# Float64 remainder bits on ScalarE, one-column softmax scaling in batch 0, and a new instruction order, in an attention and two-layer feed-forward kernel

## The chip, the cores and the metric

The kernel runs on one core of a Trainium2 chip. TensorE (PE) multiplies matrices; VectorE (DVE), ScalarE (ACT) and GpSimd (POOL) do elementwise work; SyncE (SP) issues all DMA transfers of this kernel. The metric is the device time of one execution in microseconds (us), lower being better; the median of several runs counts.

## The reference

Attention with a memory term, then two feed-forward blocks on its output. The sizes are B, H, S, D = 4, 8, 576, 64; 2304 tokens of width 512; a hidden width of 2048.

```python
scores = np.where(causal, -1e9, np.matmul(q, k.T) / sqrt(D))
a = np.exp(scores - scores.max(-1)); a /= a.sum(-1) + 1e-9
local = np.matmul(a, v)
q_p = phi(q)                       # where(x > 0, x, exp(x) - 1) + 1
mem_out = (q_p @ M_prev) / (q_p . z_prev + 1e-6)
x = g * mem_out + (1 - g) * local  # g = sigmoid(beta), per head
h = x @ moe_w_in                   # 512 -> 2048
x = where(h >= 1, h, where(h <= -1, 0, (h + 1)**2 / 4)) @ moe_w_out
h = x @ moe2_w_in
out = (max(h, 0) + alpha * min(h, 0)) @ moe2_w_out
```

The four weight matrices arrive as 64-bit floats, the scaled ones with bits beyond float32.

## The kernel before

**Precision.** The products of the feed-forward blocks run on pairs of float16: a value is split into a high and a low half, and each product is three matmuls (`mm_in`, `mm_out`). Batch 0's attention runs wholly in float32 (`plain`); its softmax weights are transposed on TensorE and copied out of PSUM into `tt`. Batches 1 to 3 split the weights into float16 pairs `p` and transpose them with a DMA (`pt<-p` in the profile). The score products `s` run in float32 in all batches, and the products after the transposes are `px`.

**Weights.** `Weights.groups` handles one of four groups of a matrix (w1i, w1o, w2i, w2o). It loads four tiles of 512 64-bit words per partition (part `a`, 512 KB each), takes maxima and scales (part `m`), and makes a float32 value of each word (parts `0` to `3`): a Prelu on ACT makes `t` from the upper 32-bit word, the lower word is shifted right by 29, and a third operation on DVE joins both. Parts `s0` and `s1` split `t` into float16 halves. `raw[:, :, 1]` is the upper word and `raw[:, :, 0]` the lower one. w2o takes another path (`flips`) that the change does not touch. The raw tiles of w1i lie in four buffers (`ring`); the float16 halves of w1o take the same four buffers afterwards. The raw tiles of w1o use buffers of tag `x` and `g`.

**Softmax.** In `attend` DVE takes the running minimum `mxt` of the negated scores into `e`, ACT makes the exponentials with their row sums `sm` (two columns, one for each head of a pair), and DVE multiplies `sm + 1e-9` with `g1i` (batch 0) or `cs` and takes the reciprocal. `p` or `pf` is `e` times that.

**Order.** Nothing is issued as written. Each call is recorded as an operation in a `Plan`; `schedule` plays the operations on modelled engines and emits them in the order of their modelled starts, engine by engine. Each engine then executes its own list in order. Among ready operations the one comes first whose section stands earlier in the list `RANK`. Section names are short: `p0` prepares batch 0, `a1C2` is the attention of batch 1, blocks C (all five), head pair 2, and `a1C2.3` its part for query block 3; `w1i0.a` are the loads of the first group of w1i; `u00` and `d00` are the first block's up and down products (`up1`, `down1`) of batch 0, chunk 0; `f00` is the second block (`ffn2`). An operation recorded with `either` may run on one of several engines: the planner keeps it on the first unless another one finishes it sooner by more than `SLACK`, or the dictionary `HOME` names the engine. `HOME` is empty before. A key is the section and the count of `either` calls in it. `Plan.cost` has a duration for each operation; `two_ports` tells which DVE operations are planned as excluding GpSimd:

```python
big = [a for a in ins if a.space != PSUM and mybir.dt.size(a.dtype) == 4 and math.prod(a.shape[1:]) > 1]
...
return method in ("tensor_tensor", "scalar_tensor_tensor") and len(big) > 1
```

All lines of the program go through a helper, so the profile puts them all at L423 (the call in `run`); tile names tell them apart.

Of the kernel before, what the change touches and what calls it, by code (L numbers as in the profile page):

```python
# [1200 lines left out]
a0A0.x2 a1C2.2 a1C2.4 u01.7 a1C2.3 a1C1.4 a1C1.3 u01.0 p1.0 d00.o3 a1C3.1 a1C1.2 p1.3 d00.o2 a1C1.0 u01.4 a1C1.1
a1C3.2 a1C3.0 u01.1 p2.0 u01.5 u01.6 a1C3.4 p2 a2C0.1 d01.o0 a1C3.3 d01.o2 a2C1.1 u10.0 d01.o1 p2.s a2C0.2 a2C1.4
a2C1.0 a2C0.q a2C1.2 w1o2.1 a2C1.3 a2C3.4 p2.1 u10.4 a2C0.3 p2.3 a2C0.0 a1C1.x4 a2C0.4 u10.6 a2C2.0 u10.7 a2C3.3
d01.o3 u10.2 a2C2.2 w1o1.3 a1C2.x4 a2C3.0 a2C3.2 a2C3.1 u10.5 u11.1 w1o2.s0 a2C2.1 u10.1 a3C0.0 a2C2.4 a2C2.3 u10.3
a0A3.x2 u11.3 a3C0.4 w1i2.a u11.6 p3.s a3C0.1 a3C0.2 d10.o0 a3C1.0 a3C1.2 w1o2.3 d10.o1 a1C1 d10.o2 a3C1.1 w1i0.s0
d10.o3 u11.2 a3C0.3 d21 w1o3.s1 u11.0 u11.5 u11.4 u11.7 d11.o0 m2.2 a2C2.x4 a0A3.q a3C1.3 a3C1.4 u20.1 u20.5 w1i3.1
a3C0.x2 d11.o2 a3C3.q d11.o1 a3C3.3 u20.4 a3C1.q d11.o3 a3C2.x2 w1i1.a s1 a3C3.4 a3C1 w2i0.a u20.0 u20.7 u20.3 u20.2
a1C2.q w1o0.0 u20.6 d20.o0 w2i0.s1 a3C1.x2 a3C2.1 d20.o2 a3C2.4 u21.2 w1o3.0 a3C2.3 u21.7 w2i0.3 a3C2.x4 a3C3.1 a3C3.2
a1C2 w2i2.a w2i0.m w1o1.2 a3C0.q a3C2.2 m3.1 u21.4 a3C2.0 a3C3.0 m2.1 d20.o1 p2.2 a1C3 w2i1.a w2i2.m d20.o3 w1o0.2
u21.3 a0A2.q w2i2.s0 w1i1.0 u21.0 a0B2.x4 u21.1 w2i2.s1 a2C1 w2i0.1 a3C3.x4 w2i2.1 u21.5 u21.6 w2i1.3 w2i3.0 d21.o2  # L1210
# [75 lines left out]
```

## Time and profile before

| | |
|---|---|
| median of 3 runs | 1060.23 us (1058.87 to 1060.51) |
| profiled execution | 1059.26 us |
| its span, first to last instruction | 1057.4 us |
| TensorE, DVE, ACT, GpSimd busy in the span | 953.8, 691.7, 560.9, 311.5 us |
| mean granted TensorE clock | 0.984 of full speed |

The profiled execution is one run with a record of each instruction. The span is 1.9 us shorter than its time, which holds what lies before the first and after the last instruction. Busy times are unions over an engine's instructions, and the stages have different limits, so the span has to be read stage by stage.

### The profile page before, as it was taken

How to read it: one execution, taken by the hardware profiler on the slowest of the kernel's cores; microseconds unless marked ns; L12 is line 12 of the kernel's file. 1: busy time of each engine (PE TensorE's matmuls, PEld its weight loads, DVE VectorE, ACT ScalarE, POOL GpSimd, SP SyncE). 2: the span in 40 equal slices, each digit the busy share in tenths (PEclk: the TensorE clock that was granted, in tenths of full speed). 3: DMA queues.
4: the chain of work that ended last, by engine and by line, in shares of the span. 5: the costliest groups of instructions: out<-in, count | busy, mean ns of one | idle time of the engine just before them, and what ended most of it. 6: DMA issues, size and time to landing. Idle time of an engine off the chain costs nothing.

```text
span 1057.4 us, 20522 instructions
## 1 busy us (share of the span) xinstructions
PE 953.8 (90%) x8043; PEld 712.8 (67%) x8043; DVE 691.7 (65%) x1777; ACT 560.9 (53%) x1099; POOL 311.5 (29%) x315
## 2 busy tenths in 40 slices
...
PEclk9999978999999999999999999999999999999999
...
GB/s 314 295 117 103 82 139 124 82 150 138 169 114 139 118 176 123 92 115 175 100 148 199 32 139 69 125 61 68 57 34 7 18 12 12 18 12 18 7 17 24
DMA packets 132097, 104.24 MB, mean 99 GB/s; under 512 B 98464, under 2 KB 113312, under 8 KB 132000
## 3 DMA queue, kind: packets, MB, share of 16 engines
...
q14 instruction: 34, 0.28, 0.1%
...
## 4 chain that ended last, share of the span: by engine, by line
PE 44%; DVE 4%; DMA 3%; ACT 1%; POOL 1%; issue 0%; ACTq 0%; SPq 0%; DVEq 0%; POOLq 0%
PE h L423 21%; PE o L423 17%; PE y L423 5%; DMA w2i_raw<-in_w2i 2%; DMA pt<-p 1%; DVE u L423 1%; PE px L423 1%; PE s L423 0%; DMA w2o_raw<-in_w2o 0%; DVE w2o L423 0%; ACT u L423 0%; POOL d L423 0%; POOL g L423 0%; DVE w2i_t L423 0%; DVE p L423 0%
## 5 line engine op out<-in xcount | busy, mean ns | idle before, releaser
L423 PE MATMUL h<-x,w1i 128*128 128x288 f16 x1536 | 202.8, 288 | 4.8 <-ACT u L423 3.4
L423 PE MATMUL y<-g,w1o 128*128 128x288 f16 x1536 | 204.2, 288 | 1.9 <-DVE ysc L423 1.8
L423 PE MATMUL o<-g,w2o 128*128 128x288 f16 x1536 | 194.7, 286 | 1.3 <-ACT u L423 0.7
L423 PE MATMUL h<-yt,w2i 128*128 128x288 f16 x1536 | 195.3, 286 | 0.1
L423 PEld LDWEIGHTS <-w1i 128*128 128x128 f16 x1536 | 147.2, 98 | 55.6 <-issue 18.0
L423 PEld LDWEIGHTS <-w1o 128*128 128x128 f16 x1536 | 146.8, 98 | 52.4 <-issue 12.8
L423 PEld LDWEIGHTS <-w2o 128*128 128x128 f16 x1536 | 150.3, 98 | 39.7 <-issue 1.9
L423 PEld LDWEIGHTS <-w2i 128*128 128x128 f16 x1536 | 150.1, 98 | 38.0 <-issue 0.3
L423 DVE SCALAR_TENSOR_TENSOR u<-u,al 128x288 f32<-128x288 f32 x128 | 66.5, 546 | 121.6 <-ACT u L423 121.5
L423 POOL TENSOR_TENSOR g<-u,g 128x576 f16<-128x576 f32 x49 | 73.4, 1501 | 211.7 <-ACT yt L423 92.9
L423 DVE TENSOR_TENSOR g<-u,g 128x576 f16<-128x576 f32 x79 | 66.7, 846 | 85.7 <-ACT g L423 85.2
L423 ACT ACTIVATE e<-e,mxt 128x64 f32<-128x64 f32 (+4 forms) x160 | 88.2, 552 | 56.0 <-DVE mxt L423 51.9
L423 PE MATMUL s<-qk 64*128 64x288 f32 (+4 forms) x384 | 90.6, 492 | 27.7 <-DVE mxt L423 12.9
L423 ACT ACTIVATE u<-h,sa 128x288 f32<-128x288 f32 x128 | 59.3, 498 | 104.6 <-PE h L423 101.3
L423 ACT ACTIVATE g<-u 128x576 f16<-128x576 f32 x117 | 79.3, 679 | 63.6 <-DVE u L423 39.9
L423 DVE SCALAR_TENSOR_TENSOR p<-e,sm,p 128x320 f16<-128x320 f32 (+4 forms) x119 | 74.1, 658 | 13.1 <-POOL p L423 7.0
L423 PEld LDWEIGHTS s<-qk 64*128 64x128 f32 x384 | 40.4, 208 | 51.8 <-DVE mxt L423 21.6
L423 DVE SCALAR_TENSOR_TENSOR u<-u,c,d 128x576 f32<-128x576 f32 x64 | 62.6, 980 | 15.2 <-ACT d L423 8.2
L423 DVE CUSTOM_DVE_ANT_0 e<-s,mask 128x64 f32<-128x64 f32 (+4 forms) x160 | 64.7, 419 | 5.4 <-PE s L423 5.1
L423 ACT ACTIVATE u<-h,bu,su 128x576 f32<-128x576 f32 x64 | 52.7, 823 | 20.5 <-PE h L423 14.6
L423 ACT ACTIVATE oe<-o,osc 128x288 f32<-128x288 f32 x32 | 16.0, 499 | 85.8 <-PE o L423 85.8
L423 ACT ACTIVATE d<-h,bu,sd 128x576 f32<-128x576 f32 x64 | 52.6, 821 | 4.9 <-PE h L423 4.8
(215 smaller groups left out, 1142.3 us busy)
## 6 DMA issues: line engine op xcount, KB each, us to landing
...
```

The source lines that it names most:

```text
L423: fn(*args, **kw)
```

## The change

A fourth constant `half` is made at the start. The new helper `rest_of` records the shift of the lower word as an operation for DVE or ACT: on ACT, the upper 16 bits of the lower word (a number below 65536) are multiplied by 2^-13, and 2^-14 - 0.5 is added, so that rounding to a whole number leaves the upper three bits, which is what the shift by 29 leaves. It is used for w1i, w1o and w2i. In batch 0 the scaling of `sm` is done for one column at a time. In the planner the rate of DMA transposes goes from 292 to 215 KB per us. `RANK` is replaced, and `HOME` gets 661 entries; of these, 33 concern `rest_of` (keys such as `w1i0.1:1`). The diff, with `RANK` and `HOME` cut to the lines that name the loads of w1i0 and w1o0 and these keys:

```diff
--- before.py
+++ after.py
@@ -15,6 +15,7 @@
 BF16 = mybir.dt.bfloat16
 I16 = mybir.dt.int16
 I32 = mybir.dt.int32
+U16 = mybir.dt.uint16
 AF = mybir.ActivationFunctionType
 ALU = mybir.AluOpType
 AX = mybir.AxisListType.X
@@ -392,7 +393,7 @@
                 busy[eng] = True
                 if eng == "dma":
                     hw = max(hw, now) + (0.625 if op.wide else 0.45)
-                    dma = max(dma, hw + 0.65) + (op.size / 360e3 if op.size > 0 else -op.size / 292e3)
+                    dma = max(dma, hw + 0.65) + (op.size / 360e3 if op.size > 0 else -op.size / 215e3)
                     if op.size < 0:
                         hw = max(hw + 0.57, dma - 0.92)
                     post(max(hw, dma - 3.0), free, eng)
@@ -563,6 +564,8 @@
         base=0,
         channel_multiplier=1,
     )
+    half = const.tile([P, 1], F32, name="half")
+    G.memset(half, 2.0**-14 - 0.5)
     gt = const.tile([P, H], F32, name="gt")
     g1i = const.tile([P, H], F32, name="g1i")
     Q.dma_start(out=gt, in_=beta.partition_broadcast(P))
@@ -593,6 +596,25 @@
             else:
                 out.append([w[:, k] for k in range(2)])
         return out
+
+    def rest_of(raw):
+
+
+        low = raw[:, :, 0]
+
+        def on_act():
+            A.activation(
+                out=low,
+                in_=raw.rearrange("p n t -> p (n t)").bitcast(U16).rearrange("p (n t) -> p n t", t=4)[:, :, 1],
+                func=AF.Identity,
+                scale=2.0**-13,
+                bias=half,
+            )
+
+        def on_dve():
+            V.tensor_scalar(out=low, in0=low, scalar1=29, scalar2=None, op0=ALU.logical_shift_right)
+
+        plan.either(on_dve, on_act)
 
     class Weights:
 
@@ -671,9 +693,7 @@
                     A.activation(out=t[:, i], in_=top.bitcast(F32), func=AF.Prelu, scale=2.0**-112, alpha=-(2.0**32))
 
                     if self.flips is None:
-                        V.tensor_scalar(
-                            out=raw[:, :, 0], in0=raw[:, :, 0], scalar1=29, scalar2=None, op0=ALU.logical_shift_right
-                        )
+                        rest_of(raw)
                     else:
                         rest3 = raw[:, :, 0].rearrange("p (f e) -> p f e", e=64)
                         V.scalar_tensor_tensor(
@@ -853,14 +873,16 @@
                     bias=mxt[:, h : h + 1],
                     accum_out=sm[:, h : h + 1],
                 )
-            V.scalar_tensor_tensor(
-                out=sm,
-                in0=sm,
-                scalar=1e-9,
-                in1=(g1i if plain else cs)[:, 2 * pr : 2 * pr + 2],
-                op0=ALU.add,
-                op1=ALU.mult,
-            )
+
+            for h in ((0, 1), (1, 2)) if plain else ((0, 2),):
+                V.scalar_tensor_tensor(
+                    out=sm[:, slice(*h)],
+                    in0=sm[:, slice(*h)],
+                    scalar=1e-9,
+                    in1=(g1i if plain else cs)[:, 2 * pr + h[0] : 2 * pr + h[1]],
+                    op0=ALU.add,
+                    op1=ALU.mult,
+                )
             V.reciprocal(out=sm, in_=sm)
             nq = P if bk else 64
             if plain:
@@ -1193,39 +1215,121 @@
 ORDER = _order()
 
 RANK = """
-s3 w1i1.1 a0A1.2 p0.1 a0A2.x2 w1i0.2 w1i0.3 m1.0 p0.s u00.0 w1i0.0 a0A1.1 w1i0.1 w1i1.m s0 a0A1.0 w1i1.s1 p0.0 w1i0.s1
-a0A0.1 c a0A1.q w1i2.1 w1i0.m a0A2.1 a0A0.q w1i2.s1 a0A0.0 p0.3 a0A2.0 a0A0.2 l p0.2 w1i2.m a0A2.2 w1o0.1 m1.3 a0A3.1
-a0A3.0 a0A3.2 a0B0.3 w1i3.m p0 p1 u00.3 w1o0.a w1o2.a u00.4 u00.5 u00.1 u00.2 a0B2.q w1o0.m w1o2.m w1o1.a u00.6 u00.7
...
-f10.4 f10.0 f10.3 f10.5 w2i3.1 w2o0.3 f11.6 w2o2.s1 a0B3 w1i0.a f10.6 f10.7 a1C1.q w2o2.3 f11.7 f11.2 t1 f10.o1
...
+w1i0.m w1i1.3 u00.0 m1.0 w1i0.s0 s0 a0A1.q d00 p0.1 w1i0.s1 a0A0.x2 w1i0.1 a0A1.0 a0A1.1 a0A0.1 p0.3 a0A0.q a0A3.q
+w1i0.a a0A0.0 p0.s w1i1.m a0A1.2 a0A0.2 a0A2.1 a0A2.0 w1i0.0 l w1i2.m a0A2.2 m1.3 p0 a0A3.0 w1o0.a w1i1.1 a0A3.1
+a0A3.2 p1 a0B0.3 w1i3.m w1i2.s1 p0.2 u00.1 w1o2.a w1o0.m u00.5 a0A3 w1o2.m w1o1.a w1i2.1 u00.7 u00.2 u00.3 w1o3.a p0.0
+u00.4 u00.6 a0B0.4 p1.2 a0B2.4 a1C0 a0B1.4 d00.o1 w1o3.m w1o0.1 w1o1.m p1.1 w1i3.0 a0B1.3 a0B2.3 a0B3.3 w1o2.s1 a0B3.4
...
 """.split()
 
-HOME = {}
+HOME = dict(
+    x.split("=")
+    for x in """
+w1i0.0:1=dve w1i0.1:1=act w1i0.s0:1=act w1i0.s0:2=dve w1i0.2:1=dve w1i0.3:1=act w1i0.s1:1=pool w1i0.s1:2=pool
...
+a0A0.x2:3=act w1i1.1:1=act w1i1.2:1=act w1i1.s1:2=pool a0A1.0:1=pool a0A1.0:2=act a0A1.0:4=act a0A1.1:1=act
+a0A1.1:4=act a0A1.2:2=act a0A1.2:3=dve a0A1.x2:1=act a0A1.x2:3=act w1i2.0:1=act w1i2.s0:1=pool w1i2.s0:2=dve
+w1i2.2:1=act w1i2.s1:1=pool w1i2.s1:2=dve a0A2.0:1=dve a0A2.0:3=pool a0A2.0:4=act a0A2.1:1=pool a0A2.1:2=pool
+a0A2.1:3=dve a0A2.2:1=act a0A2.2:2=pool a0A2.2:3=dve a0A2.2:4=act a0A2.x2:1=act w1i3.0:1=act w1i3.s0:2=dve
+w1i3.3:1=act w1i3.s1:1=act w1i3.s1:2=dve a0A3.0:1=dve a0A3.0:2=dve a0A3.0:3=pool a0A3.1:1=pool a0A3.2:2=dve
...
+u00.6:3=dve u00.7:1=act w1o0.0:1=dve w1o0.1:1=act w1o0.s0:2=dve w1o0.2:1=dve w1o0.3:1=dve w1o0.s1:1=dve w1o1.0:1=act
+w1o1.1:1=act w1o1.s0:2=pool w1o1.2:1=act w1o1.3:1=act w1o1.s1:1=pool w1o1.s1:2=dve w1o2.0:1=act w1o2.s0:1=pool
+w1o2.2:1=dve w1o2.3:1=dve w1o2.s1:1=pool w1o2.s1:2=dve w1o3.0:1=act w1o3.1:1=dve w1o3.s0:2=dve w1o3.2:1=act
...
+u21.5:3=pool u21.6:1=dve u21.6:2=act u21.7:1=act u21.7:3=dve w2i0.0:1=dve w2i0.2:1=act w2i0.3:1=act w2i0.s1:2=dve
+w2i1.1:1=act w2i1.s0:1=pool w2i1.s1:2=dve w2i2.0:1=dve w2i2.1:1=dve w2i2.2:1=dve w2i2.s1:2=dve w2i3.0:1=act
+w2i3.s0:1=act w2i3.s0:2=dve w2i3.3:1=dve w2i3.s1:1=act w2i3.s1:2=dve u30.0:2=act u30.0:3=dve u30.1:1=pool u30.1:2=pool
...
+""".split()
+)
 
 
 # ---- launch: one core; the host only lays the arrays out ----
```

## Rows read from the trace of the kernel before

**Rows 1.** The page: busy us, share of the span, count; TensorE's granted clock in slices.

```profile
PE 953.8 (90%) x8043; PEld 712.8 (67%) x8043; DVE 691.7 (65%) x1777; ACT 560.9 (53%) x1099; POOL 311.5 (29%) x315
...
PEclk9999978999999999999999999999999999999999
```

**Rows 2.** Stretches: length, busy us of PE, PEld, DVE, ACT, POOL; clock, DMA share, GB/s.

```profile
13.00:50.00 37.00, 10.53 (x48) 6.87 (x48) 32.69 (x99) 10.22 (x22) 9.76 (x8) 1.00 0.95 332
50.00:200.00 150.00, 114.57 (x741) 77.66 (x742) 132.94 (x367) 106.41 (x208) 77.84 (x69) 0.90 0.35 112
128.00:164.00 36.00, 23.77 (x136) 15.03 (x134) 29.16 (x91) 25.60 (x44) 17.37 (x16) 0.72 0.43 141
200.00:603.00 403.00, 379.51 (x3614) 272.08 (x3613) 325.15 (x939) 265.70 (x562) 180.65 (x208) 1.00 0.59 131
500.00:603.00 103.00, 99.46 (x886) 74.17 (x884) 83.64 (x189) 69.90 (x127) 42.39 (x40) 1.00 0.49 124
603.00:1057.40 454.40, 447.71 (x3640) 355.73 (x3637) 197.23 (x358) 171.80 (x296) 40.76 (x24) 1.00 0.13 42
```

**Rows 3.** TensorE's groups: count, busy us, mean ns, idle us before them, releasers.

```profile
L423 PE MATMUL s<-qk 64*128 64x288 f32 (+4 forms) x384 | 90.6, 492 | 27.7 <-DVE mxt L423 12.9 <-DMA qk<-in_qk 7.7 <-DVE w1o_t L423 3.4
L423 PE MATMUL px<-pt,vh 128*64 128x128 f16 (+1 forms) x1080 | 40.3, 219 | 15.1 <-DMA pt<-p 12.0 <-DVE x L423 1.4 <-PE h L423 0.7
L423 PE MATMUL pt<-ident,pf 128*128 128x128 f32 x120 | 24.4, 354 | 17.4 <-ACT pf L423 12.3 <-POOL pf L423 5.0
L423 PE MATMUL px<-tt,vf 128*64 128x128 f32 (+1 forms) x240 | 23.0, 337 | 8.0 <-ACT tt L423 5.7 <-ACT e L423 2.3
```

**Rows 4.** DVE's groups by shape: batch 0's scaling of `sm`, the three shifts by 29.

```profile
L423 DVE SCALAR_TENSOR_TENSOR sm<-sm,g1i 128x2 f32<-128x2 f32 x20 | 10.2, 509 | 2.5 <-ACT e L423 2.3
...
L423 DVE TENSOR_SCALAR w1o_raw<-w1o_raw 128x512 int32<-128x512 int32 x16 | 7.9, 492 | 1.8 <-DMA w1o_raw<-in_w1o 1.8
...
L423 DVE TENSOR_SCALAR w2i_raw<-w2i_raw 128x512 int32<-128x512 int32 x16 | 7.5, 471 | 0.2 <-DMA w2i_raw<-in_w2i 0.2
L423 DVE TENSOR_SCALAR ring<-ring 128x512 int32<-128x512 int32 x16 | 7.2, 455 | 1.0 <-DMA ring<-in_w1i 0.9
```

**Rows 5.** ACT's groups by shape: plain copy, bias from a tile, Prelu of raw words.

```profile
L423 ACT ACTIVATE g<-u 128x576 f16<-128x576 f32 x117 | 79.3, 679 | 63.6 <-DVE u L423 39.9 <-PE o L423 21.3 <-PE y L423 2.2
...
L423 ACT ACTIVATE d<-d,c 128x576 f32<-128x576 f32 x51 | 39.3, 771 | 0.7
...
L423 ACT ACTIVATE w1i_t<-ring 128x512 f32<-128x512 f32 x16 | 10.5, 666 | 9.0 <-POOL w1i L423 4.8 <-DMA ring<-in_w1i 2.4 <-DVE w1i L423 1.8
```

**Rows 6.** The tiles `sm` and `mx`: operation, count, ns min/median/max, first and last start.

```profile
L423 DVE SCALAR_TENSOR_TENSOR sm<-sm,g1i x20: 145/157/2068, 11.2 to 183.7; 128x2 f32<-128x2 f32 x20
...
L423 DVE TENSOR_TENSOR mx<-rm,sq x16: 147/156/1044, 17.0 to 425.4; 128x1 f32<-128x1 f32 x16
```

**Rows 7.** The timeline: start us, duration us, around three of these operations.

```profile
59.31 2.13 POOL L423 TENSOR_TENSOR w1i<-w1i_t,w1i 128x1024 f16<-128x1024 f32 x1
...
59.53 1.93 DVE L423 SCALAR_TENSOR_TENSOR sm<-sm,g1i 128x2 f32<-128x2 f32 x1
...
63.52 0.14 DVE L423 SCALAR_TENSOR_TENSOR sm<-sm,g1i 128x2 f32<-128x2 f32 x1
63.59 0.21 DVE L423 CUSTOM_DVE_ANT_0 e<-s,mask 128x64 f32<-128x64 f32 x1
...
421.87 1.55 POOL L423 TENSOR_TENSOR g<-u,g 128x576 f16<-128x576 f32 x1 [0.66 <-ACT g L423]
...
422.40 1.04 DVE L423 TENSOR_TENSOR mx<-rm,sq 128x1 f32<-128x1 f32 x1
```

**Rows 8.** The DMA issues: count, median us from issue to landing.

```profile
pt<-p SPq DMA_TRANSPOSE x60, 4.3
```

**Rows 9.** The timeline of SP, which issues the transfers.

```profile
5.56 4.12 SPq L423 DMA_DIRECT2D w1o_raw<-in_w1o  x5
...
10.40 0.55 SPq L423 DMA_DIRECT2D ring<-in_w1i  x1
```

More of the change, by code (lines that the diff above doesn't have):

```diff
@@ L1201 @@
[L1201 to L1210, printed above, removed]
@@ new lines @@
+a1C2.2 u01.1 a1C2.4 a1C2.1 a1C3.1 d00.o3 w1i3.3 a1C3.0 s3 a1C1.1 a1C1.0 a1C3.2 a1C1.2 a2C0.1 p1.3 d10 w1o0.3 a1C3.4
+a0B1 a1C3.3 w1o1.s0 w1o2.1 d00.o2 u01.4 u01.0 p2.s u01.6 d01.o1 w1i1.s0 u01.5 w1i1.s1 d01.o0 a2C1.2 a2C1.1 u10.4
+a2C1.0 w1o1.2 a2C0.2 a2C1.3 a2C1.4 a2C0.4 a2C0.3 d01.o3 a2C3.3 a2C3.0 d01.o2 a2C0.0 u10.6 a2C3.4 u10.1 u10.0 a2C2.1
+a2C3.2 u10.2 a2C3.1 u10.3 a2C2.0 w1o1.0 p2.0 u10.5 u11.1 u10.7 d10.o0 a2C2.4 d10.o1 a2C2.2 a2C2.3 w1o3.2 a3C0.0 a3C1.3
+u11.6 m3.0 d10.o2 u11.3 a3C0.1 p3.s w1o0.0 a3C1.4 w1i3.s1 d10.o3 d21 u11.5 w1o3.s0 u11.7 a3C0.2 w2i0.0 m3.2 u11.0
@@ new lines @@
+a3C0.x4 a3C1.0 u11.2 u11.4 d11.o0 d11.o1 m1.2 w2i0.a a0B2.x4 a3C0.4 a3C0.3 w1i1.0 d11.o3 u20.3 a3C3.4 a3C1.1 u20.4
+w1i0.2 m3.1 a3C1.2 a1C2.q w1i3.s0 p2 a3C2.2 a1C2 a3C1 w1i2.3 u21.2 a3C2.1 w2i0.1 a3C3.q d11.o2 a2C0.q u20.7 a0B2
+a3C2.x2 m1.1 u20.0 w2i0.s1 a2C0.x2 a3C2.4 m2.1 a3C3.3 u21.3 w2i2.s1 a0A2.x2 a3C2.0 u20.5 w1i2.s0 d11 u20.1 a3C3.1
+w2i0.m a3C1.x2 u20.2 u21.7 a3C2.x4 a2C0.x4 u20.6 a3C0.q a3C3.0 a2C2.q w2i2.0 a2C1.q u21.4 d20.o0 d20.o3 p2.3 w1i0.3
+w1o3.s1 d20.o1 u21.5 d20.o2 a3C3.2 a1C1 a1C0.x2 u21.1 w2i2.a a3C2.3 w2i1.s0 w2i3.3 u21.0 u21.6 w2i2.m d21.o0 w2i1.s1
@@ new lines @@
+w2i1.a d21.o1 u30.1 d21.o2 a1C1.x4 d21.o3 u30.0 u30.6 u31.2 w2i2.2 m3.3 w2i3.a w1o1.1 w2i2.s0 w2i1.2 w2i3.s0 w1i3.a
+f01 u30.4 w2i3.m c u30.2 u30.7 a2C3.x2 u30.3 m2.2 u31.1 w1o1.3 w2o3.a w1o2.3 w2i2.1 p2.1 w2i1.m u30.5 w2o0.1 u31.5
+d30.o2 d30.o0 w2o3.m f00 w1o0.s0 w2o0.a d30.o1 d30.o3 w2o3.3 a1C3 w2o3.2 u31.0 a2C0 w2i1.3 w2o0.m w2i3.2 w2o1.m u31.7
+w1o2.2 p2.2 a3C1.q u31.3 u31.4 f00.2 f00.3 u31.6 f00.7 a2C1 d31.o1 f00.6 w2o2.2 s1 d31.o0 w2o0.s0 d31.o3 w2o3.s0
+d31.o2 w2o3.s1 w1i2.a f00.1 a2C3 w1o1.s1 a2C2 w1o3.3 f00.4 f00.0 a0A0 f01.7 f00.5 f01.5 f01.6 p3.1 d01 d30 f00.o1
```

93 lines of the change are left out of this document (77 added, 16 removed).

## The prediction, as put on record before the changed kernel was timed

> **What bounds the kernel now.** I read the page first. TensorE is busy for 953.8 of the 1057.4 us, so 103.6 us are idle; VectorE (DVE) comes second with 65%, and the granted clock is at full speed except in a few slices [rows 1]. An average over unlike stages says little, so the stages come next. From 603 us to the end TensorE is idle for only 454.4 - 447.7 = 6.7 us: nothing but fewer matmuls could shorten that part, and the change removes none. Between 200 and 603 it is idle for 23.5 us, between 50 and 200 for 35.4 us, and between 13 and 50 for 26.5 us [rows 2]. A gain has to come out of the first 603 us, mostly out of the first 200. There DVE is busy for 32.69 + 132.94 = 165.6 of 187 us, which is 0.89, while ScalarE (ACT) is at 106.4 of 150, which is 0.71 after 50 us. So up to 200 us DVE is nearly the bound; at 500 to 603 us TensorE is. The worst hole is 128 to 164 us: 12.2 us idle, at a mean granted clock of 0.72, so part of it ran at the lower of the two levels, 1.2 GHz [rows 2]. Third, the groups of TensorE with the idle time before them say what was late: score products wait for DVE's running minima, the transposes of batch 0 for ACT (12.3 us), the products after a DMA transpose for that transpose (12.0 us), and those after a copy out of PSUM for ACT (8.0 us) [rows 3].
>
> **The change part by part.** The sum is made against the profiled execution, 1059.3 us; the median of the runs shown is 1.0 us above it.
>
> *The shift on ACT.* `rest_of` may run on DVE or on ACT; 48 tiles pass through it, 16 each of w1i, w1o and w2i. The list `HOME` pins 33 of them: 8 on ACT and 2 on DVE for w1i, 8 and 6 for w1o, 4 and 5 for w2i; the planner chooses for the other 15, with DVE as the home it leaves only for a clear gain. I count the 20. On DVE one takes 455, 492 and 471 ns by mean [rows 4], so 8 x 0.455 + 8 x 0.492 + 4 x 0.471 = 9.4 us leave DVE. With none of the free 15 on DVE it would be 14 x 0.455 + 10 x 0.492 + 11 x 0.471 = 16.5 us. On ACT the new operation has no row. The nearest is the Prelu of the same 512 words at 666 ns, and a bias read from a tile adds 771 - 679 = 92 ns at equal width [rows 5]: 0.76 us each, 15.2 us in all, bounds 0.67 (a free bias) to 0.85 (twice that addition). What is this worth on the path? The 16 of w1i and w1o (7.6 us of DVE) stand before 200 us, where DVE is 0.89 busy: 7.6 x 0.89 = 6.7 us gained. The four of w2i fall where TensorE idles 3.5 of 103 us [rows 2]; the full TensorE queue hides them, and without that cover they would bring their 1.9 us. Against it stand 16 x 0.76 = 12.2 us more on ACT. Operations queued behind them are the copies for which TensorE waits; such waits (12.3 + 8.0 us, the latter partly the exponentials) fill about 20.3 of 150 us, so I charge 12.2 x 0.135 = 1.7 us. Net: -5.0 us. Bounds: -6.7 with ACT's room hiding all, +12.2 with every one in front and no relief on DVE.
>
> The Trainium skill ("ScalarE: Activation LUTs", Rules for kernel authors) sends adds and products to VectorE and not to ScalarE. By that rule the exchange costs 0.76 - 0.47 us of engine time per tile, 5.8 us over the 20; the sum would have +5.8 in place of -5.0. The rule looks at an engine alone; here the engine it prefers is the fuller one.
>
> *One column at a time.* The scaling of the softmax sums of batch 0 becomes two instructions of one column for one of two. That is 20 more on DVE. An unhindered one took 0.14 us and let the next operation begin 0.07 us after its own start [rows 7], so 20 x 0.07 x 0.89 = +1.2 us, and with 0.15 each +2.7. Can it bring something? The 20 take 145 ns at least, 157 at the median and 2068 at most; with a mean of 509 (10.2 us over 20) they hold 20 x (509 - 157) = 7.0 us too much [rows 4, 6]. Four long ones (1.5 to 2.07 us) carry nearly all of it, each beside a GpSimd operation: the one at 59.53 ended with GpSimd's product of 59.31 [rows 7]. If one column ended these stalls, 7.0 x 0.89 = 6.3 us would come back. But the trace has an operation with two inputs of one column, `mx<-rm,sq`. It has a median of 156 ns and once took 1044: it began at 422.40 and ended at 423.44, while GpSimd's product began at 421.87 and ended at 423.42 [rows 6, 7]. So one column waited for GpSimd too. I take 0 for the gain, with -6.3 as the other end.
>
> The Trainium skill ("SBUF — State Buffer", Who interferes with whom) says that a DVE instruction with two SBUF inputs contends with a GpSimd instruction that reads SBUF, and names no width below which it does not. By that rule the sum keeps +1.2; the planner's own test in `two_ports` leaves out operands of one column, and by that the sum would have 1.2 - 6.3. The long `mx` is on the rule's side.
>
> *Landing times.* The 60 DMA transposes are 12 of each of five block lengths, 131 KB times 1 to 5, so 393 KB on average. The planner had 0.625 + 0.65 + 393/292 + 0.8 = 3.4 us for it, and now has 393/215 instead: 3.9 us. The trace has 4.3 us from issue to landing [rows 8]. The plan was 0.9 us short and is now 0.4 us short, so it should put more other work before the products. The waits are 12.0 us; a bit over half would be 6, and I take -5.0, as other work has to be found for each; bounds 0 to -12.0.
>
> *New order.* `w1i0.a` now ranks before `w1o0.a`. Before, five loads of w1o (512 KB each) left SP's queue from 5.56 us, and the first of w1i followed at 10.40 [rows 9]; nothing needs w1o until the first `down1`. What stands behind them in SP's queue moves too: the loads of `vc`, from which `prepare` takes its scale, then find four loads of w1i ahead of them in place of five of w1o, about as much. Five loads at the 332 GB/s of this stretch [rows 2] are 7.9 us; DVE idles only 4.3 us there, so I take -2.0, bounds 0 to -4.3. All other places in `RANK` and the pins in `HOME` have no row: the plan is a list from a model, and a step that is put behind a late one delays all behind it in its in-order queue. I take 0, between -12.2 (the hole at 128 us filled) and the same on the other side (a second hole of that size).
>
> **Sum:** -5.0 + 1.2 - 5.0 - 2.0 = -10.8 us. 1059.3 - 10.8 = 1048.5; with the 1.0 us to the median, 1049 us. A difference under 0.2% (2.1 us) counts as none: single runs lie 1.6 us apart.
>
> **The rivals.** *The split works* (chance 0.10): one column escapes GpSimd, 1049 - 6.3, about 1043 us. For it: 16 of 20 sums did not stall at all, so a new place may do the same. Against: the long `mx`.
>
> *The hole closes* (0.15): the new order brings `down1` of batch 0 into the stretch at 128 to 164 us. The hole holds 12.2 us of idleness, and 0.28 x 23.8 = 6.7 us went to the clock; half of the 18.9 us gives about 1040 us. For it: the low clock lies in the hole itself, so work put there would pay twice. Against: DVE is 0.81 busy there and w1o itself has to be prepared by it.
>
> *Nothing arrives* (0.10): ACT takes what DVE gives, and the transposes were covered only in name; 1060 us. For it: the freed DVE time is under 6% of the first 200 us. The Trainium skill's rule above (ScalarE: Activation LUTs) points here: with its +5.8 the sum ends at 1060.3 us.
>
> *ACT becomes the bound* (0.20), the other side: the moved shifts stand ahead of the copies `tt`, `pf` and of the drains of `h`, between 98 and 164 us where ACT is already 0.71 busy. The whole +12.2 us counts and the relief of DVE brings nothing: 17.2 us more than my sum, 1067 us. It decides as soon as about eight of the 16 stand in front of an awaited copy (8 x 0.76 = 6.1 us, without relief), because the other three terms, 1.2 - 5.0 - 2.0 = -5.8, are then outweighed.
>
> **How the numbers follow.** My sum has 0.42 and a range of its own of 1041 to 1057; 0.03 stay for larger shifts. Faster: 0.42 + 0.10 + 0.15 and a little of "nothing arrives", 0.68. Same 0.10. Slower: 0.20 and a little, 0.22. The range from 1034 to 1067 leaves out the low end of "the hole closes" and the upper half of "ACT becomes the bound", with the larger shifts about 0.18.
>
> **What would show it.** In the changed profile ACT should have some 20 or more activations from the raw tile of 0.67 to 0.85 us, and DVE as many shifts fewer. The 40 one-column sums should have a median near 0.15 us, with some still over 1 us beside a GpSimd product. TensorE's idle time before 200 us should be some 8 us shorter, its waits for transposes near 7 us, and the stretch after its attention work unchanged. I am wrong if idle time before ACT's copies grows, if the granted clock falls in a second stretch, or if the order leaves a later hole.

## The result and the profile after

The changed kernel takes 1043.15 us (median of 4 runs, 1039.10 to 1045.69) against 1060.37 us (4 runs, 1058.87 to 1060.94) for the kernel before on the same chip. The ratio is 0.9839, 95% interval 0.9809 to 0.9868: it is faster by 17.2 us. The forecast was 1049 us with a range of 1034 to 1067, and 0.68 for faster. The profiled execution took 1042.5 us, its span 1040.6 us.

The page of the changed kernel, the rows that answer to [rows 1]:

```profile
PE 947.1 (91%) x8043; PEld 709.2 (68%) x8043; DVE 684.7 (66%) x1803; ACT 515.6 (50%) x1030; POOL 375.7 (36%) x405
...
PEclk9999988999999999999999999999999999999999
```

TensorE does the same 8043 products in 6.7 us less, at a mean granted clock of 0.993 in place of 0.984, and it is idle for 1040.6 - 947.1 = 93.5 us in place of 103.6. These two, less product time and less idle time, are the whole 16.8 us of span. What one would not have guessed from the words of the change is the other end of the row: GpSimd is 64 us busier and ACT 45 us less busy, although ACT received work.

The stretches after, as in [rows 2]:

```profile
13.00:50.00 37.00, 8.65 (x37) 5.63 (x37) 33.42 (x106) 19.21 (x44) 13.08 (x13) 1.00 0.92 325
50.00:200.00 150.00, 123.95 (x841) 84.56 (x842) 133.64 (x397) 109.26 (x210) 72.70 (x68) 0.95 0.37 120
128.00:164.00 36.00, 26.21 (x152) 16.00 (x148) 32.16 (x98) 28.28 (x53) 20.27 (x17) 0.81 0.34 114
200.00:603.00 403.00, 383.06 (x3659) 275.93 (x3657) 332.22 (x949) 246.86 (x524) 225.34 (x262) 1.00 0.59 132
603.00:1040.60 437.60, 431.49 (x3511) 343.03 (x3508) 180.52 (x344) 134.13 (x245) 63.07 (x55) 1.00 0.12 40
```

Idle time of TensorE is the length less its busy time: 28.4 us at 13 to 50 (1.9 more than before), 26.1 at 50 to 200 (9.4 less), 19.9 at 200 to 603 (3.6 less), and 6.1 in the rest, which stayed as it was. The hole at 128 to 164 is still there: 9.8 us idle in place of 12.2, clock 0.81 in place of 0.72.

A second way to read the same gain is to count TensorE's instructions up to a moment. Three stretches, first of the kernel before:

```profile
0.00:200.00 200.00, 126.54 (x793) 85.03 (x794) 169.28 (x482) 123.35 (x242) 90.12 (x85) 0.92 0.49 161
200.00:400.00 200.00, 182.08 (x1791) 128.04 (x1790) 160.44 (x513) 129.99 (x302) 87.86 (x110) 0.99 0.67 142
400.00:603.00 203.00, 197.43 (x1824) 144.04 (x1824) 164.71 (x427) 135.71 (x260) 92.78 (x99) 1.00 0.51 121
```

and of the changed kernel:

```profile
0.00:200.00 200.00, 132.60 (x878) 90.20 (x879) 171.94 (x511) 134.60 (x262) 87.29 (x90) 0.97 0.50 168
200.00:400.00 200.00, 188.77 (x1884) 131.47 (x1882) 171.46 (x522) 127.10 (x295) 131.80 (x168) 1.00 0.68 150
400.00:603.00 203.00, 194.28 (x1775) 144.46 (x1775) 160.76 (x428) 119.76 (x229) 93.54 (x94) 1.00 0.50 115
```

The changed kernel is 85 instructions ahead at 200 us, 178 at 400 and 129 at 603. At 447.71 / 3640 = 0.123 us each [rows 2] that is an estimate of 10, 22 and 16 us. The instructions differ in length, so a second estimate goes by the busy time of TensorE that is still to come: at 200 us it is 953.8 - 126.5 = 827.3 us before and 947.1 - 132.6 = 814.5 after, a lead of 13 us, and in the same way 19 us at 400 and 16 at 603. So half of the lead or somewhat more is made in the first 200 us, as forecast; another 7 to 11 us come between 200 and 400 us, where the forecast saw only the transposes; and some of it is lost again later.

The groups of TensorE after, as in [rows 3]:

```profile
L424 PE MATMUL s<-qk 64*128 64x288 f32 (+4 forms) x384 | 89.7, 481 | 15.8 <-DVE mxt L424 14.2 <-DMA qk<-in_qk 1.3
L424 PE MATMUL px<-pt,vh 128*64 128x128 f16 (+1 forms) x1080 | 39.9, 220 | 9.9 <-DMA pt<-p 6.9 <-DVE x L424 2.6
L424 PE MATMUL pt<-ident,pf 128*128 128x128 f32 x120 | 24.1, 349 | 20.4 <-POOL pf L424 16.1 <-ACT pf L424 4.2
L424 PE MATMUL px<-tt,vf 128*64 128x128 f32 (+1 forms) x240 | 24.0, 341 | 7.6 <-ACT tt L424 6.7 <-DVE tt L424 0.9
```

Scores wait 11.9 us less in all; for the minima alone they wait a little longer (14.2 against 12.9 us), while the waits for `qk` and `w1o_t` are mostly gone. The products after a DMA transpose wait 6.9 us for it in place of 12.0. The transposes of batch 0 wait somewhat longer than before, and for GpSimd where it was ACT. The 16.1 us are nearly all one wait at the start. In the timeline (start, duration, engine, and in brackets the idle time before), `ph` is a product of batch 0's preparation:

```profile
37.47 3.55 POOL L424 TENSOR_TENSOR ph<-qn,zb 128x640 f32<-128x640 f32 x2 [4.75 <-DMA vf<-in_vp]
38.72 2.31 DVE L424 SCALAR_TENSOR_TENSOR sm<-sm,g1i 128x1 f32<-128x1 f32 x3
...
41.21 0.32 POOL L424 TENSOR_SCALAR pf<-e,sm 128x64 f32<-128x64 f32 x1 [0.19 <-DVE sm L424]
...
41.59 0.69 PE L424 MATMUL pt<-ident,pf 128*128 128x128 f32 x2 [15.68 <-POOL pf L424]
```

The copy that ends the wait takes 0.32 us itself. Before it GpSimd makes two products `ph` until 41.02, and DVE's sums last until then too. So the releaser's name alone says little here; experiments 5 and 10 come back to this.

The tiles of the edits after: count, ns min/median/max, first and last start.

```profile
L424 DVE SCALAR_TENSOR_TENSOR sm<-sm,g1i x40: 131/150/1796, 38.7 to 169.4; 128x1 f32<-128x1 f32 x40
...
L424 ACT ACTIVATE ring<-ring,half x12: 731/764/782, 11.3 to 57.6; 128x512 int32<-128x512 uint16 x12
...
L424 ACT ACTIVATE w1o_raw<-w1o_raw,half x9: 739/763/790, 18.5 to 142.8; 128x512 int32<-128x512 uint16 x9
...
L424 ACT ACTIVATE w2i_raw<-w2i_raw,half x9: 759/773/822, 258.6 to 578.7; 128x512 int32<-128x512 uint16 x9
```

Thirty shifts run on ACT (12 + 9 + 9), 18 stay on DVE, and one takes 0.76 to 0.77 us, as priced. The sums have their median at 150 ns and still reach 1796 ns. The timeline shows the longest of them:

```profile
129.87 2.12 POOL L424 TENSOR_TENSOR w1o<-w1o_t,w1o 128x1024 f16<-128x1024 f32 x1
...
130.22 1.80 DVE L424 SCALAR_TENSOR_TENSOR sm<-sm,g1i 128x1 f32<-128x1 f32 x1
...
131.94 0.44 DVE L424 CUSTOM_DVE_ANT_0 e<-s,mask 128x288 f32<-128x288 f32 x1
```

A sum of one column started 0.35 us after GpSimd's product and ended (132.02) when that product ended (131.99), and the next minimum on DVE started only then. By the trace 18 of the 40 sums overlap a GpSimd instruction, and eleven of these take 292 to 1796 ns; the 22 that overlap none take 131 to 161 ns.

What did the new assignments move? The groups of GpSimd and of ACT answer that:

```profile
L424 POOL TENSOR_TENSOR p<-e,p 128x64 f16<-128x64 f32 (+4 forms) x40 | 33.3, 832 | 3.3
...
L424 POOL TENSOR_SCALAR e<-e,sm 128x64 f32<-128x64 f32 (+4 forms) x40 | 26.1, 652 | 23.8 <-ACT p L424 13.8 <-DVE p L424 7.4 <-ACT g L424 2.0
```

```profile
L424 ACT ACTIVATE g<-u 128x576 f16<-128x576 f32 x61 | 41.6, 681 | 43.8 <-DVE u L424 23.2 <-PE o L424 19.4 <-PE y L424 1.1
```

Forty of the 120 low halves of the probabilities of batches 1 to 3 (`rest`, which makes `e` times `sm` less the upper half) are now made on GpSimd, 33.3 + 26.1 = 59.4 us of work; in the kernel before, 119 of them were one DVE instruction each. And 56 of the 117 copies `g` left ACT [rows 5]; 37 of them went to GpSimd and 19 to DVE.

### The profile page after: what moved, and what is told of

Same layout as the page of the kernel before. It is cut to its first block, busy times and chain, and to the rows that moved or that the text cites. A ratio compares the mean times of both kernels' runs of the same rounds, so it can differ in the third digit from the quotient of the medians.

```text
span 1040.6 us, 20570 instructions
## 1 busy us (share of the span) xinstructions
PE 947.1 (91%) x8043; PEld 709.2 (68%) x8043; DVE 684.7 (66%) x1803; ACT 515.6 (50%) x1030; POOL 375.7 (36%) x405
## 4 chain that ended last, share of the span: by engine, by line
PE 40%; DVE 4%; DMA 3%; POOL 2%; issue 2%; ACT 1%; SPq 0%; ACTq 0%; POOLq 0%
PE h L424 21%; PE o L424 17%; PE y L424 3%; DMA pt<-p 1%; DMA w2o_raw<-in_w2o 1%; DVE u L424 1%; DMA w2i_raw<-in_w2i 1%; POOL d L424 1%; POOL w2o L424 0%; DVE p L424 0%; ACT u L424 0%; DVE yt L424 0%; DMA yr<-y 0%; POOL p L424 0%; ACT d L424 0%
## 5 line engine op out<-in xcount | busy, mean ns | idle before, releaser
L424 PE MATMUL h<-x,w1i 128*128 128x288 f16 x1536 | 200.5, 286 | 4.6 <-ACT d L424 2.1
L424 POOL TENSOR_TENSOR g<-u,g 128x576 f16<-128x576 f32 x54 | 74.1, 1372 | 182.7 <-ACT g L424 132.6
L424 ACT ACTIVATE e<-e,mxt 128x576 f32<-128x576 f32 (+4 forms) x160 | 88.3, 553 | 65.6 <-DVE mxt L424 55.1
L424 POOL TENSOR_SCALAR g<-u 128x576 f16<-128x576 f32 x40 | 30.5, 764 | 213.4 <-DVE u L424 156.9
L424 PE MATMUL s<-qk 64*128 64x288 f32 (+4 forms) x384 | 89.7, 481 | 15.8 <-DVE mxt L424 14.2
L424 DVE TENSOR_TENSOR g<-u,g 128x576 f16<-128x576 f32 x74 | 59.9, 810 | 31.5 <-ACT g L424 18.7
L424 DVE SCALAR_TENSOR_TENSOR u<-u,c,d 128x576 f32<-128x576 f32 x64 | 59.7, 934 | 14.4 <-POOL d L424 10.1
L424 DVE CUSTOM_DVE_ANT_0 e<-s,mask 128x288 f32<-128x288 f32 (+4 forms) x160 | 64.3, 419 | 6.6 <-PE s L424 4.2
L424 ACT ACTIVATE u<-h,bu,su 128x576 f32<-128x576 f32 x64 | 52.8, 825 | 21.8 <-PE h L424 16.6
L424 ACT ACTIVATE g<-u 128x576 f16<-128x576 f32 x61 | 41.6, 681 | 43.8 <-DVE u L424 23.2
L424 DVE SCALAR_TENSOR_TENSOR p<-e,sm,p 128x320 f16<-128x320 f32 (+4 forms) x80 | 57.0, 730 | 8.2 <-POOL p L424 5.8
```

The lines of the kernel that those rows point to most:

```text
L424: fn(*args, **kw)
```

## The experiments

In those that say "lists kept", every engine executes the instructions of its kernel in the places that its plan gave them; only the edited ones are issued in another form, through a field `emit` of the operation:

```diff
-                for fn, args, kw in op.ways[eng][0]:
+                for fn, args, kw in op.ways[eng][0] if op.emit is None else op.emit:
```

Those that say "planned anew" change something that the planner reads. Each ratio is to the kernel before on the same chip.

**1. after_shift_dve: the changed kernel with the shift on DVE, lists kept.**

```diff
-        plan.either(on_dve, on_act)
+        op, full = plan.either(on_dve, on_act)
+        op.emit = full["dve"][0]
```

The thirty shifts that the plan gives to ACT are issued on DVE, at their time in the plan.

> The changed kernel with the same order on every engine, but the 30 remainder shifts that ran on ScalarE are issued on VectorE, each at the place in the order where it stood. Theory (the shift is worth about what the prediction charged, 5 us): 23 of the 30 lie before 200 us where VectorE is nearly full, so 1043 + 5 = 1048 us, with VectorE busy 30 x 0.42 = 12.6 us longer before its waits. Rival 1 (the order alone makes the gain): within 2 us of 1043. Rival 2 (the shift makes most of the gain): 1055 us or more. Rival 3 (ScalarE was delayed by it): faster than 1041.

Measured: 1049.94 us, ratio 0.9904 (0.9888 to 0.9919). The interval lies above that of the changed kernel, so in the new order the shift on ACT is worth 6.8 us by the medians. A second pair says the same: experiments 6 and 3 below, both with the sums whole, differ only in the shift too, by 10.7 us (1050.47 and 1039.74).

```profile
L427 PE MATMUL s<-qk 64*128 64x288 f32 (+4 forms) x384 | 93.1, 492 | 18.9 <-DVE mxt L427 16.7 <-DMA qk<-in_qk 1.4 <-DVE w1o L427 0.5
```

The scores wait 2.5 us longer for the minima, which DVE makes. Summed over all of its waits, TensorE waits 55.4 us for DVE here and 48.2 in the changed kernel (with whole sums 55.6 and 46.9): that is the relief that was meant. Its price is to be seen as well, in the waits for ACT's copies (us in total, times, longest):

```profile
PE px L427 <- ACT tt L427: 4.1, 6, 1.1
PE pt L427 <- ACT pf L427: 3.6, 2, 3.3
```

With the shift on ACT these are 6.7 and 4.2 us, 3.2 us longer. The rest of the 6.8 us lies in TensorE's busy time, 947.1 us in the changed kernel and 951.5 here; why it differs is not shown. One thing the run leaves open: the lists were made for a kernel with the shift on ACT, and a plan made for it on DVE could win back a part of the 6.8 us. None was tried.

**2. before_shift_act: the same thirty shifts on ACT in the kernel before, lists kept** (`upper16` stands for the view that `rest_of` reads).

```diff
+                        if plan.name in ON_ACT:
+                            plan.ops[-1].emit = [(nc.scalar.activation, (), dict(out=raw[:, :, 0], in_=upper16,
+                                func=AF.Identity, scale=2.0**-13, bias=half))]
```

> The kernel before, order unchanged, with the same 30 remainder shifts on ScalarE as in the changed kernel, each at the place in the global order where VectorE had it; nothing else is changed. Theory (freed VectorE time before 200 us is worth about 0.9 of itself, as 6.8 us in the new order): 1060 - 5 = 1055 us, with the first feed-forward product 3 us earlier than 98.1. Rival (the shift helps only in an order made for it): within 2 us of 1060, with longer waits of TensorE for ScalarE's copies. Rival (ScalarE becomes the bound): 1063 us or more.

Measured: 1064.09 us, ratio 1.0027 (1.0011 to 1.0044): no gain, rather a loss of some 3 us (1.2 to 4.7 by the interval). That is where the rival with ACT as the bound begins.

```profile
128.00:164.00 36.00, 22.50 (x131) 14.32 (x128) 23.59 (x83) 27.85 (x48) 15.44 (x15) 0.72 0.44 141
```

```profile
L425 PE MATMUL s<-qk 64*128 64x288 f32 (+4 forms) x384 | 89.3, 490 | 27.2 <-DVE mxt L425 13.8 <-DMA qk<-in_qk 10.9 <-DVE ym L425 1.4
L425 PE MATMUL px<-pt,vh 128*64 128x128 f16 (+1 forms) x1080 | 40.6, 221 | 15.9 <-DMA pt<-p 14.4 <-PE h L425 0.7 <-DVE x L425 0.4
L425 PE MATMUL pt<-ident,pf 128*128 128x128 f32 x120 | 23.6, 346 | 17.9 <-ACT pf L425 13.7 <-POOL pf L425 4.1
```

In the hole DVE is busy for 23.6 us in place of 29.2, ACT for 27.9 in place of 25.6, and TensorE did less, not more [rows 2]. DVE's room stands there unused, which I read so: each engine's next instruction is the one that the old plan put there, and it waits for something else. Summed over all of TensorE's waits, those for DVE fall from 47.5 to 42.2 us, while those for ACT grow from 25.9 to 29.8 and those for transfers from 19.7 to 25.3. So the relief is there and others take it. The trace of experiment 4, whose time is that of the kernel before, has 46.1, 26.5 and 23.5 us; the growth for transfers is thus partly the spread from run to run, and which wait costs the 3 us is not shown.

**3. after_sum_whole: the changed kernel with batch 0's sums as one instruction of two columns, lists kept.**

```diff
+            if plain:
+                plan.ops[-2].emit = []
+                plan.ops[-1].emit = [(nc.vector.scalar_tensor_tensor, (), dict(out=sm, in0=sm, scalar=1e-9,
+                    in1=g1i[:, 2 * pr : 2 * pr + 2], op0=ALU.add, op1=ALU.mult))]
```

> The changed kernel with the same order on every engine, but each pair of one-column sum scalings is one instruction of two columns at the place of the second. Theory (one column waits for GpSimd as two do): the 20 instructions keep stalls of 1 to 2 us, their total falls from 14.2 us to some 10 us, and the time is 0 to 3 us below 1043. Rival (the split does end stalls): more or longer stalls than in the changed kernel, total over 14 us, and the time 3 to 6 us above 1043.

Measured: 1039.74 us, ratio 0.9828 (0.9801 to 0.9854). It overlaps the changed kernel's interval: the split brings nothing that shows, and whether it costs some 3 us can't be told. The stalls stay, up to 1777 ns:

```profile
L425 DVE SCALAR_TENSOR_TENSOR sm<-sm,g1i x20: 142/162/1777, 38.3 to 167.0; 128x2 f32<-128x2 f32 x20
```

**4. before_split: the kernel before with the sums split, lists kept** (two instructions of one column in place of the one of two).

> The kernel before, every engine's list kept, with batch 0's twenty two-column sums written as two one-column sums in the same place. If a one-column sum waits for GpSimd like a two-column one (the prediction's reading), the forty take 13 to 17 us of VectorE in place of 10.2, single ones last over 1 us beside a GpSimd instruction, and the time is that of the kernel before or up to 4 us more. If one column at a time avoids the wait (the rival that the split works), none lasts over 0.3 us, the forty take about 6 us, and the time falls by 3 us or more.

Measured: 1060.95 us, ratio 1.0003 (0.9984 to 1.0021): no difference.

```profile
L424 DVE SCALAR_TENSOR_TENSOR sm<-sm,g1i x40: 140/151/2066, 11.2 to 183.3; 128x1 f32<-128x1 f32 x40
```

One column waits up to 2066 ns, like two columns [rows 6]. In the groups by shape the forty take 3.2 us more than the twenty [rows 4], and the time does not show it:

```profile
L424 DVE SCALAR_TENSOR_TENSOR sm<-sm,g1i 128x1 f32<-128x1 f32 x40 | 13.4, 367 | 2.0 <-ACT e L424 2.0
```

**5. after_sum_pointer: the changed kernel with the sums in a form whose factor is read as one value for each partition, lists kept.**

```diff
+                if plain:
+                    plan.ops[-1].emit = [(nc.vector.tensor_scalar, (), dict(out=sm[:, slice(*h)], in0=sm[:, slice(*h)],
+                        scalar1=1e-9, scalar2=g1i[:, 2 * pr + h[0] : 2 * pr + h[1]], op0=ALU.add, op1=ALU.mult))]
```

> The changed kernel with the same order, but the 40 one-column scalings are tensor-scalar instructions: one tensor input, and the factor read as a per-partition scalar. Theory (the wait for GpSimd comes with the second tensor input, not with the width): none of the 40 over 0.3 us, total 6 to 7 us in place of 14.2, and the time 3 to 6 us below 1043. Rival (any read of the batch's factor waits): stalls over 1 us stay, and the time is within 2 us of 1043.

Measured: 1043.17 us, ratio 0.9847 (0.9823 to 0.9872): the time of the changed kernel. The tile, and the timeline beside the same GpSimd product as above:

```profile
L425 DVE TENSOR_SCALAR sm<-sm,g1i x40: 192/203/217, 39.7 to 172.9; 128x1 f32<-128x1 f32 x40
```

```profile
130.58 2.13 POOL L425 TENSOR_TENSOR w1o<-w1o_t,w1o 128x1024 f16<-128x1024 f32 x1
...
130.93 0.21 DVE L425 TENSOR_SCALAR sm<-sm,g1i 128x1 f32<-128x1 f32 x1 [0.17 <-ACT e L425]
```

The stalls are gone: by the trace 23 of the 40 overlap a GpSimd instruction, and none takes over 217 ns. So the long sums wait because of their form (a second tensor as input), not because of their width. But 6 us less of DVE (7.8 us for the forty in place of 13.7, by shape) moved the median by nothing; the intervals leave room for a gain of some 5 us. The wait at the start shows one place where the removed stall buys little:

```profile
38.44 3.56 POOL L425 TENSOR_TENSOR ph<-qn,zb 128x640 f32<-128x640 f32 x2 [4.51 <-DMA vf<-in_vp]
39.68 0.45 DVE L425 TENSOR_SCALAR sm<-sm,g1i 128x1 f32<-128x1 f32 x3
...
41.98 0.32 POOL L425 TENSOR_SCALAR pf<-e,sm 128x64 f32<-128x64 f32 x1
42.34 0.47 PE L425 MATMUL pt<-ident,pf 128*128 128x128 f32 x1 [15.40 <-POOL pf L425]
```

The first sums are done at 40.13, but GpSimd's copy `pf` stands behind the products `ph` in GpSimd's own list and comes at 41.98. From the start of `ph` to TensorE's transpose it takes 3.90 us in place of 4.12. Elsewhere the gain is not accounted for: the scores wait 2.2 us less for the minima, and TensorE's clock in the first 200 us was 0.92 in place of 0.97 in this execution, which took 1047.83 us.

**6. after_order_only: both edits undone in place in the changed kernel, lists kept** (1 and 3 together).

> The changed kernel's order with both edits of instructions undone at their places (30 shifts on VectorE, sums of two columns): what is left is the new order and the engines that were assigned. Theory: order and assignment make about two thirds of the gain, 1047 us. Rival (the shift makes it): 1055 us or more. Rival (order alone makes all of it): 1043 us.

Measured: 1050.47 us, ratio 0.9911 (0.9897 to 0.9925). The order with its assignments is worth 9.8 us by itself (1060.29 for the kernel before in these runs), 8 to 11 by the interval.

```profile
0.00:200.00 200.00, 128.70 (x829) 86.61 (x830) 172.38 (x499) 116.98 (x232) 83.76 (x85) 0.95 0.50 165
200.00:400.00 200.00, 189.64 (x1856) 132.24 (x1854) 169.63 (x518) 126.45 (x295) 132.52 (x169) 1.00 0.68 148
```

Here TensorE is 36 instructions ahead of the kernel before at 200 us and 101 at 400; by the busy time still to come (951.0 us in all) that is 5 and 13 us, where the changed kernel had 13 and 19. So the lead that is made between 200 and 400 us is there with the order and its assignments alone; what the changed kernel has beyond it is made in the first 200 us, where 21 of its 30 shifts on ACT belong (w1i and w1o).

**7. after_no_home: the changed kernel with `HOME = {}`, planned anew.**

> The changed kernel without the 661 assigned engines: same list, same edits, the planner picks engines itself. Theory (list and assignments share the order's 10 us): 1047 to 1050 us, with GpSimd's busy time back from 376 to about 310 us. Rival (the list does it all): within 2 us of 1043. Rival (list and assignments only work together): 1055 us or more.

Measured: 1100.21 us, ratio 1.0375 (1.0328 to 1.0423), 57 us slower than with the pins and 40 slower than the kernel before. The low halves go back to DVE (119 of them), and two groups and the first stretch show where TensorE loses:

```profile
L424 PE MATMUL s<-qk 64*128 64x288 f32 (+4 forms) x384 | 88.2, 481 | 28.4 <-DVE mxt L424 24.5 <-DMA qk<-in_qk 2.5 <-DVE w1i_am L424 0.8
...
L424 PE MATMUL pt<-ident,pf 128*128 128x128 f32 x120 | 24.3, 354 | 25.9 <-ACT pf L424 19.8 <-POOL pf L424 5.8 <-DVE pf L424 0.3
...
0.00:200.00 200.00, 113.04 (x704) 75.54 (x705) 151.21 (x449) 125.48 (x243) 88.45 (x84) 0.89 0.46 155
```

At 200 us it is 174 instructions behind the changed kernel. The 57 us are not the price of the pins alone: to leave them out is to plan anew, and experiment 9 shows what that costs with the pins kept.

**8. before_rate215: the kernel before with the planner's rate at 215e3, planned anew.**

```diff
-op.size / 292e3
+op.size / 215e3
```

> The kernel before with one number changed, the planner's rate for DMA transposes, 215 in place of 292; the planner then makes its order anew from the old list. Theory (the true landing times alone are worth some 5 us): 1055 us, and TensorE's idle time before the products that follow a DMA transpose falls from 12.0 to about 7 us. Rival (the rate is worth something only with a list that was made with it): within 3 us of 1060, even if that idle time falls, since it returns at other waits.

Measured: 1070.27 us, ratio 1.0094 (1.0066 to 1.0122): 10 us slower, which neither expectation had. TensorE waits longer for the transposes than with the short landing times, 15.3 us against 12.0 [rows 3] (13.5 in experiment 4, where the order is that of the kernel before):

```profile
L423 PE MATMUL px<-pt,vh 128*64 128x128 f16 (+1 forms) x1080 | 40.4, 220 | 19.1 <-DMA pt<-p 15.3 <-DVE x L423 2.6 <-DVE mx L423 1.1
```

**9. after_rate292 and after_rate169: the changed kernel with the rate back at 292e3, and as far off on the other side, planned anew.**

> The changed kernel with the planner's rate for DMA transposes put back to 292; list and assignments stay. Theory (the landing times carry about half of the order's 10 us): 1048 us, with TensorE's idle time before the products after a DMA transpose up from 6.9 to 10 us or more. Rival (the list alone keeps the transposes early enough): within 2 us of 1043 and the idle time under 8 us.

> The changed kernel with the planner's rate for transposing transfers at 169e3, as far from 215e3 in time for each byte as 292e3 was on the other side; list and assignments stay, the plan is made anew. If the loss at 292e3 came from landing times that were too early (the rate itself is what is right), slower landing times in the plan lose little: 1043 to 1048 us, and TensorE's wait for the transposes stays under 8 us. If the list and the assignments were found together with 215e3 and any other plan misses their fit, it loses 8 us or more on this side too (1051 to 1075 us), also where no transpose is waited for.

Measured: 1066.04 us at 292e3, ratio 1.0044 (1.0022 to 1.0065), and 1067.73 us at 169e3, ratio 1.0064 (1.0038 to 1.0089). The same two groups, first at 292e3:

```profile
L424 PE MATMUL s<-qk 64*128 64x288 f32 (+4 forms) x384 | 88.0, 482 | 15.9 <-DVE mxt L424 13.9 <-DMA qk<-in_qk 1.1 <-DVE qn L424 0.7
L424 PE MATMUL px<-pt,vh 128*64 128x128 f16 (+1 forms) x1080 | 40.6, 221 | 19.4 <-DMA pt<-p 15.9 <-DVE x L424 1.7 <-DMA vh<-vh 1.5
```

and at 169e3:

```profile
L424 PE MATMUL s<-qk 64*128 64x288 f32 (+4 forms) x384 | 91.7, 499 | 26.5 <-DVE mxt L424 22.8 <-DMA qk<-in_qk 2.8 <-DVE ys_m L424 0.7
L424 PE MATMUL px<-pt,vh 128*64 128x128 f16 (+1 forms) x1080 | 41.0, 224 | 5.7 <-DMA pt<-p 4.0 <-DMA vh<-vh 1.4 <-DVE x L424 0.2
```

With this list, the longer the planned landing time, the shorter the wait for transposes: 15.9, 6.9 and 4.0 us at 292, 215 and 169. Yet the time is 23 us worse on the one side and 25 us worse on the other, where the transposes are waited for least. At 169 the scores wait 8.6 us longer for the minima. By the forecast's sum, 169 stands for 0.625 + 0.65 + 393/169 + 0.8 = 4.4 us of landing, which is nearer to the 4.3 of the trace [rows 8] than the 3.9 of 215. So the loss at 169 is not one of wrong landing times, and at 292 only a part of it can be (9.0 us more waiting for transposes). I read it so: the list and the pins fit one plan, and the other plans tried, those of 292, of 169 and of no pins, miss it.

**10. after_pf_act: the changed kernel with GpSimd's fourteen copies `pf` issued on ACT, lists kept, and after_pf_act_whole, the same with the sums whole.** TensorE's 16.1 us of waiting for GpSimd's `pf` looked like a price of the pins.

```diff
-                    copy(p[:, h, :w], e[:, h, :w], sm[:, h : h + 1], (A, V, G))
+                    op, full = copy(p[:, h, :w], e[:, h, :w], sm[:, h : h + 1], (A, V, G))
+                    op.emit = {"pool": full["act"][0]}
```

> The changed kernel, every engine's list kept, but for the fourteen copies that scale batch 0's probabilities on GpSimd, which are issued on ACT at their time in the plan. TensorE waits 16.1 us for GpSimd's part of those tiles in the changed kernel. If that wait is a price of the new assignments that sets the start, ACT's 0.56 us in place of 0.64 us and fewer GpSimd instructions beside VectorE's sums shorten it by 5 us or more and the time falls by 3 to 8 us. If the assignments fit the order, ACT's chain takes the wait over: TensorE waits for ACT's copies instead, and the time is 1043 to 1050 us.

> The same with the sums of batch 0 as one two-column instruction again. If the copies off GpSimd bring time, the two together are the fastest version: 1034 to 1040 us. If not, it takes 1040 to 1048 us, like the changed kernel with whole sums.

Measured: 1047.83 us, ratio 0.9883 (0.9851 to 0.9915), and 1046.00 us, ratio 0.9858 (0.9828 to 0.9888). Neither is faster than the changed kernel; the first is slower by 4.7 us, with intervals that just overlap. The wait has only changed its name, 22.5 us where GpSimd and ACT had 16.1 + 4.2:

```profile
L427 PE MATMUL pt<-ident,pf 128*128 128x128 f32 x120 | 25.0, 358 | 22.5 <-ACT pf L427 22.5
```

Its longest part, 17.1 us, is the one at the start. There DVE's sums still last until the products `ph` end (42.42 us), and ACT copies after them. Experiment 5 took away the stall of the sums and left the copy behind `ph`; this one moved the copy and left the stall. The two together were not tried.

## Why the forecast held, and what in it did not

**The total.** The likeliest case, 1041 to 1057 us, holds the 1043 us; the median is 5.9 us under its 1049. That 1043 is also the figure given for the rival "the split works" is a coincidence: experiments 3 to 5 show that the split brought nothing. And that the sum came out is in part luck: two of its terms, the shift and the landing times, were worked out on rows of the kernel before, and put into that kernel alone both come out with the other sign (+3 and +10 us).

**The shift on ACT (-5.0).** Measured -6.8 us in the new order; by the ends of the two intervals of experiment 1 it lies between 2 and 12 us. The price of one, 0.76 us, was right; there are 30 and not the 20 counted. In the new order the mechanism is the forecast's: TensorE's waits for DVE fall by 7.2 us (forecast 6.7), its waits for ACT's copies grow by 3.2 (forecast 1.7). Against it as a price of the edit stands experiment 2: in the old order the same thirty cost 3 us. DVE's waits fall there too, by 5.3 us, but other waits take that and more. The rival "ACT becomes the bound" had the right sign for the old order, at a quarter of its 12.2 us, and did not occur in the new one. The rule that the forecast weighed, from the Trainium skill ("ScalarE: Activation LUTs", Rules for kernel authors), additions and products to VectorE, agrees with the single-engine times here (0.76 us on ACT against 0.46 to 0.49 on DVE [rows 4]) and with the loss in the old order, and not with the time of the changed kernel.

**One column at a time (+1.2).** The reading of the long `mx` was right: one column waits for GpSimd as two do (1796 and 2066 ns). The price is not to be seen: 0 in the old order, 3 us by the medians in the new, within its noise. Even removing the stalls altogether (experiment 5) gave nothing that shows.

**Landing times (-5.0).** The wait fell by 5.1 us, from 12.0 to 6.9, as forecast. But the step "so it should put more other work before the products" did not hold by itself: in the old list the same edit made the wait longer and the kernel 10 us slower (experiment 8), and in the new one 169, the truer landing time, is 25 us slower (experiment 9).

**New order (-2.0, and 0 for the rest).** Here is the term that was mis-sized. Order, pins and landing times together measured -9.8 us (experiment 6) where the forecast had -5.0 - 2.0 + 0 = -7.0. The early loads of w1i did not shorten the start: TensorE's idle time at 13 to 50 us rose by 1.9 us and DVE's fell only from 4.3 to 3.6. What the forecast charged at 0, all other places and the pins, cannot be left out: planned anew without the pins the kernel is 57 us slower (experiment 7), and they are what moved the low halves off DVE and the copies off ACT. The lead that is made between 200 and 400 us is there without the shift and the split (experiment 6). GpSimd is busy for 131.8 us in place of 87.9 in that stretch, so it lies where the moved work lies. That it comes from those moves, and not from other places in the list, was not tried by itself.

**The sum of the parts.** -6.8 for the shift, about 0 for the split and -9.8 for order and pins make -16.6 of the 17.2 us measured. But each was measured with the rest in its final place, and with the sums whole the shift is worth 10.7. Put into the kernel before one at a time, the shift gave +3, the split 0, the rate +10. What list and pins made anew for the kernel without the shift on ACT would reach, no run shows.

**The other rivals.** "The hole closes" did not occur: at 128 to 164 us 9.8 of 12.2 us of idle time remain, and by the rival's own sum the 12.2 + 6.7 = 18.9 us became 9.8 + 0.19 x 26.2 = 14.8, 4.1 us gained and not nine. "Nothing arrives" is excluded by the interval.

**What was to be seen.** Right: the activations from the raw tiles, the sums, the waits for transposes (forecast near 7, measured 6.9), idle time from 13 to 200 us 7.5 us shorter (forecast some 8), and the unchanged last stretch. The signs of being wrong stayed away: TensorE's waits for ACT's `pf` and `tt` fell from 18.0 to 10.9 us, and the granted clock fell in no new stretch. Not foreseen: the move to GpSimd, and the lead from 200 to 400 us.

No version here beats the changed kernel beyond doubt; that with whole sums (1039.74 us) is level with it.
